# A new hand-written opening of six units, and a background planner with new costs, in a spectral filter plus gated MLP kernel

## The chip, the cores and the metric

The kernel runs on one core of a Trainium2 chip. The metric is the device time of one execution in microseconds (us); less is better. Engines are named as in the profile: PE is the matmul engine (TensorE), PEld its weight loads, DVE the vector engine, ACT the scalar engine, POOL the GpSimd engine, SP the engine whose queue issues the DMA transfers here.

## The reference

The input `x` has 2048 rows of 448. It is normalised along its rows, and three things are added: `x`, a filter in the frequency domain, and a gated MLP without bias.

```
xn = layernorm(x)                       # 2048 x 448
X  = rfft2(xn) * (w_r + 1j*w_i)         # 2048 x 225 complex
A  = irfft2(X, s=(2048, 448))
gate, up = xn @ W_gate, xn @ W_up       # 448 -> 1792
B  = (relu(gate) * up) @ W_down         # 1792 -> 448
out = x + A + B
```

## The kernel before

**Number format.** Every matrix product is made of fp16 products: an operand is split into a high part (its fp16 rounding) and a low part (the rest), and three products are summed: high by high, high by low, low by high. The low parts are made on DVE, most of the high parts on ACT. Weights are scaled by powers of two that come from their sums of squares: squares on ACT (`w_sq`, L661), the sum over partitions on POOL (`w_sum`, L666, a `partition_all_reduce`), the scale on DVE (`w_scale`, L671), then the high part on ACT (`w_hi`, L679) and the low part on DVE (`w_lo`, L683).

**Rows and chunks.** The 2048 rows are 16 blocks of 128, numbered n2. Four blocks form a chunk q (n2 = q, q+4, q+8, q+12); chunks are taken in the order 0, 2, 1, 3. A block is loaded (`load_xr`), its statistics taken on DVE (`ln_stats`), normalised, split into the tile `tt`, and transposed into `T{q}`, which holds the chunk with features on the partitions. For chunk 0 the transposes are matmuls with an identity (`ln_tp`, L328) into a PSUM tile `fx` and evictions (`ln_ev`, L334); for the others they are DMA transposes on the SP queue (`ln_dma`, L323).

**Units.** The hidden size 1792 is 14 slabs f of 128, in groups of 5, 5 and 4. A `gu` unit is one slab and one chunk: gate and up, 20 matmuls of 512 columns (`gu_full`, L728) and a pass of half-height matmuls that is shared by two units that stand next to each other, "mates" (`gu_halves`, L756). The unit's two PSUM tiles come from a ring of two (`gu`), so unit k+2 waits until unit k has been read. After it come relu on ACT (`gu_relu`), gate times up on DVE (`gu_times`), the high part of h on ACT (`gu_hi`) and the low part on DVE (`gu_lo`). When a group's slabs are done for a chunk, four `dn` units follow, one for each block: the down projection, 15 or 12 matmuls of 448 columns (`dn_mm`, L791), and an accumulation on DVE (`dn_post`, L803).

**The opening.** The first stretch is an order written by hand: the text `OPENING` (L30) is a list of pieces, and each piece's instructions go to their engines in that order, without any rescheduling. The names carry the work:

- `lx`, `ly`, `lw`, `lwd`, `lid`, `lfd`: transfers on SP of a block of x (for the norm, for the result), of the next weight slab, of a down slab, the identity, the DFT matrix
- `st`, `sq`/`rs`, `xn`, `hi`, `cp`, `lo`, `dm`: statistics; reciprocal root (A for blocks 0 and 4, B for 8 and 12, C for the second chunk); normalise; high part; a small copy on POOL; low part; DMA transpose
- `tpA`/`tpB`, `vev`/`aev`: three and five PE transposes of a block, and their eviction on DVE (v) or ACT (a)
- `wsq`, `par`, `wsc`, `whi`, `wlo`: the five weight steps, of slab `W0` to `W4`, gate `g0` and up `g1`
- `hh`, `lh`, `hl` with two digits: for slab 0, the products high by high, low by high and high by low, for gate or up (first digit) and one half of the chunk's columns (second digit, 256 columns)
- `gu1g0` and the like: a whole half unit, ten matmuls of 512 columns; `hp0`: the half-height pass of slab 0 and its mate
- `re`, `tm`, `gh`, `gl`: the four steps after a unit
- `wdq`, `wdp`, `wdsc`, `wdh`, `wdl`: the same steps for the down slabs
- `warm`, `kw1`, `kw3`, `kw6`: matmuls of 512 columns on a zeroed tile (`keep_warm`, L1052; `NWARM` = 19 for `warm`), whose result is not used

**After the opening** a loop goes over the unit list `units` (L989 to L998, L1147). A scheduler that simulates the engines sets the order in which the instructions stand in each engine's queue; units and their order in the list are priorities for it, not an order. Each unit is given weight steps and transfers at fixed distances before they are needed (`sched`, L1008 to L1046), and a share of the *background*: the list `bg` of all DFT steps, in order, each with a cost in us of DVE time and some with PE time (`PE_US`, L837). A unit may take background worth `room(i, share)`: its own length (`took`, L1121) times a share, less DVE work that it has anyway (`fixed`, L1124). The share is the smallest with which all the background fits (L1132 to L1138).

Of the kernel before, what the change touches and what calls it, by code (L numbers as in the profile page):

```python
# [30 lines left out]
lx0 lx4 lw lid lw lx8 lx12 lw lw lw lw lx2 lx10 lx6 lx14 lwd0 lwd1 lwd2 lwd3 lwd4 warm st0 st4 sqA rsA hi4  # L31
xn4 xn0 wsqW0g0 cp4 st8 hi0 parW0g0 st12 wsqW0g1 cp0 tpA0 lo0 tpA4 kw1 wscW0g0 sqB tpB0 kw6 parW0g1 wsqW1g0
rsB whiW0g0 vevB0 lo4 wsqW1g1 xn12 tpB4 kw3 hi8 parW1 wscW0g1 xn8 whiW0g1 cp8 vevA0 vevA4 hi12 tpA8 vevB4
hh10 hh00 lo8 wsqW2g1 cp12 tpA12 hl00 lo12 aevA12 tpB8 aevA8 hl10 wloW0g0 lw aevB8 tpB12 wscW1 lh00 aevB12
wloW0g1 lw lfd hh01 hh11 whiW1g0 st2 lh01 lh10 whiW1g1 hl01 wloW1g0 lw hl11 wsqW2g0 wloW1g1 lw ly0 ly4 ly8
ly12 lh11 wsqW3g0 st10 parW2 hp0 st14 wsqW3g1 gu1g0 st6 wdq0 parW3 wscW2 sqC wscW3 whiW2g0 rsC gu1g1 re0
wloW2g0 whiW3g1 tm0 whiW2g1 xn6 wsqW4g0 xn2 gu2g0 wloW2g1 hi2 re1 xn10 gh0 wloW3g1 whiW3g0 tm1 gu2g1 wdq1
wloW3g0 hi10 xn14 lo2 hi14 hi6 cp14 hp2 wsqW4g1 cp2 lo6 gu3g0 cp10 dm2 lo14 re2 parW4 wdq2 cp6 wscW4 tm2
whiW4g0 dm14 lo10 wdq4 gu3g1 wloW4g0 gh1 dm10 gl0 whiW4g1 gl1 dm6 gu4g0 re3 wloW4g1 wdq3 tm3 wdp gh3
wdsc gh2 gu4g1 gl2 wdh1 wdh2 wdl1 wdh0 wdl2 hp4 gl3 re4 wdh3 tm4 wdl0 gh4 wdh4 gl4 wdl3 wdl4  # L40
"""
# [41 lines left out]
def _constants():  # L83
# [49 lines left out]
    for r in (0, 2, 1, 3):  # L133
# [4 lines left out]
    c_fm = c_fm.reshape(4, 4, 128, 2, 128).transpose(1, 2, 0, 3, 4)  # L138
    ident = np.eye(128, dtype=np.float16)
    return dict(ident=ident, c_fd=c_fd, c_fm=np.ascontiguousarray(c_fm), c_im=c_im, c_row=c_row,  # L140
                c_id=np.ascontiguousarray(c_id))


@with_exitstack
def tile_gfnet_reglu(ctx: ExitStack, tc: tile.TileContext, x, xr, wgu, wd, wf, ident, c_fd, c_fm, c_im, c_row, c_id,
                     out):
# [181 lines left out]
    def ln_tp(n2, tiles):  # L328
        if n2 not in tp:
            tp[n2] = fx().bitcast(F16).rearrange("p (a b) -> p a b", b=128)  # L330
        for a in tiles:
            P.transpose(tp[n2][:, a, :], tt[n2][:, a, :], id_t)
# [394 lines left out]

    def gu_full(f, q, gs, cs, start, stop, seq=SEQ):  # L728
        for g in gs:
            for i, (a, b) in enumerate(seq):  # L730
                last["P"] = P.matmul(hps[f, q][:, g, cs], wt[f, g][:, a, :], Tq[q][:, b, cs],  # L731
                                     start=(start and i == 0), stop=(stop and i == len(seq) - 1)).ins

    def gu_half(f, q, g, start, prev):


        rows, b = TOP[g]
        m = P.matmul(hps[f, q][:, g, 0:512], wt[f, g][rows, 7, :], Tq[q][rows, b, :], start=start, stop=not start).ins  # L738
# [103 lines left out]
    def ln_chunk(q):  # L842
        for j in range(4):
            add(0.79, ln_stats, q, j)
        add(0.0, ln_sd, q)
        add(0.75, ln_rstd, q, (0, 1, 2, 3), True)
        n = [q + 4 * j for j in (0, 2, 1, 3)]
        for t in range(4 + 2):
            for st, (c, fn) in reversed(list(enumerate(((0.0, ln_norm), (0.78, ln_lo), (0.0, ln_dma))))):
# [5 lines left out]
    fl = ((0.0, f_dft), (0.77, f_eo), (1.08, f_x), (0.63, f_lo), (0.0, f_sdft), (None, f_y1))  # L855
    bf = (1.26, 2.04, 2.04, 2.04, 1.56, 2.04, 2.04, 2.04)

    def fft_chunk(q):
        n = [q + 4 * j for j in (0, 2, 1, 3)]
        for t in range(4 + len(fl) - 1):  # L860
            for st in reversed(range(len(fl))):
                i = t - st
                if 0 <= i < 4:
                    add(fl[st][0] if st < 5 else 1.25 * (n[i] >= 8), fl[st][1], n[i])

# [57 lines left out]
    for i0 in range(10):  # L923
# [15 lines left out]
        for k in pair_k:  # L939
            add(2.04, wmul, k)  # L940
# [76 lines left out]

    for f in groups[1] + groups[2]:
        s = first[f]
        for g in range(2):  # L1020
            sched(gslot(s, 7), w_sq, f, g)
        sched(gslot(s, 7), w_sum, f)
        sched(gslot(s, 5), w_scale, f)
        for g in range(2):
            sched(gslot(s, 4), w_hi, f, g)
            sched(gslot(s, 4), w_lo, f, g)
            sched(gslot(s, 4), load_wn)
    for i in range(8):
# [23 lines left out]
    def keep_warm(n):  # L1052
        for _ in range(n):
            P.matmul(wps, warm[:, 0:128], warm, start=True, stop=True)

    pieces = {"lid": lambda: nc.sync.dma_start(id_t, ident), "lfd": lambda: nc.sync.dma_start(fd_t, c_fd),
              "lw": load_wn, "warm": lambda: keep_warm(NWARM),
              **{f"kw{n}": (lambda n=n: keep_warm(n)) for n in (1, 3, 6)},
              "wdp": lambda: wd_sum(len(groups[0])),
# [24 lines left out]

    for f in groups[0]:
        piece(f"lwd{f}", load_wd, f)
        piece(f"wdq{f}", wd_sq, f, f)
        piece(f"wdh{f}", wd_hi, f, f)
        piece(f"wdl{f}", wd_lo, f, f)
        piece(f"parW{f}", w_sum, f)  # L1090
# [5 lines left out]
        for g in range(2):  # L1096
# [4 lines left out]
            if f == 0:  # L1101
                piece(f"parW{f}g{g}", w_sum, f, (g,))
                piece(f"wscW{f}g{g}", w_scale, f, (g,))
                for h in range(2):
                    for tag, sq in (("hh", seq1[0:3]), ("lh", seq1[3:6]), ("hl", seq2)):
                        piece(f"{tag}{g}{h}", gu_full, f, q, (g,), half[h], tag == "hh" and h == 0, False, sq)

    with tc.manual_schedule(engines={mybir.EngineType.PE, mybir.EngineType.DVE, mybir.EngineType.Activation,
                                     mybir.EngineType.SP, mybir.EngineType.Pool}):
        A.activation(mt([128, 1], F32, "root"), eps, AF.Sqrt)  # L1110
        G.memset(warm, 0.0)
        wps = psum.tile([128, 512], F32, name="dn", bufs=2)
# [33 lines left out]

    for i, u in list(enumerate(units))[len(groups[0]):-4]:  # L1147
        is_gu = u[0] == "gu"
# [7 lines left out]
        with after(LAG):  # L1156
# [6 lines left out]
            run_bg(amount=room(i, load[0]) if i >= RAMP else 0.0)  # L1163
        if is_gu:
# [57 lines left out]
```

## Time and profile before

| | |
|---|---|
| three timed runs | 446.81, 447.11, 447.32 us (median 447.11) |
| the profiled execution | 447.5 us, span 445.7 us |
| instructions | 7367 |
| busy, share of the span | PE 98%, DVE 87%, ACT 42%, POOL 6% |
| granted PE clock | full in all 40 slices |
| DMA | 39.54 MB, mean 89 GB/s |

The profile is of one execution. Its span runs from the first to the last instruction; the device time has some 2 us more around it. Lines such as L731 are lines of the kernel; a row of the timeline has the start in us from the span's start, the duration in us, the engine, the line, the operation, what it writes and reads, the count of instructions that were merged into the row, and in brackets the idle time of the engine before it and what ended it. A matmul's end is modelled and overlaps the next one's start, so the distance between starts says what a matmul costs.

### The profile page before, as it was taken

The numbers are of one execution on the slowest core, as the hardware profiler recorded it, in microseconds if no ns is written. First come the engines' busy times: TensorE is split into PE (matmuls) and PEld (weight loads), VectorE is DVE, ScalarE is ACT, GpSimd is POOL, SyncE is SP. The second block draws the span as 40 slices with busy tenths as digits, with TensorE's granted clock in tenths as the row PEclk, the third lists the DMA queues.
The fourth block names the chain that finished last, engine by engine and source line by source line (L and its number), as shares of the span: only waits on it lengthen the run. The fifth ranks groups of instructions, "written<-read, shape, count | busy, mean of one in ns | idle before, by whom it ended". The sixth has DMA issues, their size and how long they took to land.

```text
span 445.7 us, 7367 instructions
## 1 busy us (share of the span) xinstructions
PE 438.1 (98%) x2625; PEld 219.4 (49%) x2625; DVE 386.9 (87%) x958; ACT 187.0 (42%) x398; POOL 27.7 (6%) x77
## 2 busy tenths in 40 slices
PE   6999999999999999999999999999999999999997
PEld 2644645455445444444444444444454555555654
DVE  5999779786969999899999999999979799699753
ACT  4897263642552975133114354253323134144230
POOL 4220011200100040000000010000000000000000
PEclk9999999999999999999999999999999999999999
DMA  7919995400001272422220210002011211201212
GB/s 249 338 50 252 304 355 106 96 0 17 8 1 48 96 226 80 128 61 83 85 84 2 83 42 1 1 1 73 12 48 47 70 34 56 89 28 53 96 63 82
DMA packets 37756, 39.54 MB, mean 89 GB/s; under 512 B 16550, under 2 KB 33624, under 8 KB 37720
## 3 DMA queue, kind: packets, MB, share of 16 engines
q1 hardware_dynamic: 37720, 39.09, 28.3%
q8 instruction: 20, 0.33, 0.3%
q14 instruction: 16, 0.13, 0.1%
HBM read 24.38 MB, written 3.67 MB: 63 GB/s over the span
## 4 chain that ended last, share of the span: by engine, by line
PE 79%; DVE 9%; DMA 5%; ACT 3%; issue 1%; SPq 1%; DVEq 0%; ACTq 0%
PE gu L731 44%; PE dn L799 22%; PE gu L738 3%; PE fx L630 2%; PE fx L649 2%; PE fx L361 2%; PE fx L398 2%; DMA wf<-in_wf 1%; DMA sw<-y 1%; DMA y<-in_xr 1%; ACT junk L186 1%; PE dn L819 1%; ACT wt L681 1%; PE gu L819 1%; DVE wt L685 1%
## 5 line engine op out<-in xcount | busy, mean ns | idle before, releaser
L731 PE MATMUL gu<-T,wt 128*128 128x512 f16 (+1 forms) x1140 | 255.0, 375 | 0.0
L731 PEld LDWEIGHTS <-wt 128*128 128x128 f16 x1140 | 108.7, 98 | 128.7 <-issue 8.9
L799 PE MATMUL dn<-wdt,h 128*128 128x448 f16 x624 | 127.6, 353 | 0.1
L799 PEld LDWEIGHTS <-h 128*128 128x128 f16 x624 | 60.2, 98 | 57.7 <-issue 0.8
L768 ACT ACTIVATE g<-gu 128x512 f32<-128x512 f32 x56 | 33.0, 590 | 82.4 <-PE gu L738 55.6
L776 ACT ACTIVATE h<-g 128x512 f16<-128x512 f32 x56 | 35.1, 628 | 76.8 <-DVE g L772 73.8
L772 DVE SCALAR_TENSOR_TENSOR g<-gu,g 128x512 f32<-128x512 f32 x56 | 38.3, 684 | 4.2 <-ACT g L768 4.1
L780 DVE TENSOR_TENSOR h<-g,h 128x512 f16<-128x512 f32 x56 | 38.3, 685 | 3.7 <-ACT h L776 3.4
L805 DVE SCALAR_TENSOR_TENSOR xy<-dn,dsc,xy 128x448 f32<-128x448 f32 x44 | 29.9, 679 | 6.3 <-PE dn L799 6.2
L614 ACT ACTIVATE vt<-y,fsc 128x456 f16<-128x456 f32 x16 | 10.8, 673 | 26.1 <-PE fx L630 13.3
L654 DVE SCALAR_TENSOR_TENSOR xy<-fx,fsc,xy 128x448 f32<-128x448 f32 x16 | 10.8, 680 | 11.8 <-PE fx L649 11.7
L681 ACT ACTIVATE wt<-wst,wsc 128x512 f16<-128x512 f32 x28 | 19.2, 715 | 3.8 <-DVE wsc L196 3.8
L685 DVE SCALAR_TENSOR_TENSOR wt<-wst,wsc,wt 128x512 f16<-128x512 f32 x28 | 20.5, 747 | 0.1
L189 POOL PARTITION_ALL_REDUCE wm<-wm x15 | 7.8, 518 | 179.6 <-ACT junk L186 175.5
L186 ACT ACTIVATE junk<-wst 128x512 bf16<-128x512 f32 x28 | 17.5, 624 | 1.0 <-DMA wst<-in_wgu 0.7
L738 PE MATMUL gu<-T,wt 64*128 64x512 f16 x112 | 17.0, 381 | 0.2 <-DVE wt L685 0.2
L535 DVE TENSOR_TENSOR y<-y,sw 128x228 f32<-128x228 f32 x32 | 12.5, 390 | 5.0 <-DMA sw<-y 4.9
L405 DVE TENSOR_TENSOR y<-y,y 128x456 f32<-128x456 f32 x22 | 13.8, 629 | 1.7 <-DMA row<-y 1.4
L392 DVE TENSOR_TENSOR Xh<-X,Xh 128x456 f16<-128x456 f32 x16 | 10.0, 628 | 5.6 <-ACT Xh L389 5.5
L404 DVE TENSOR_TENSOR y<-y,y 128x456 f32<-128x456 f32 x22 | 13.9, 630 | 0.3
L389 ACT ACTIVATE Xh<-X 128x456 f16<-128x456 f32 x16 | 9.3, 578 | 10.1 <-DVE X L387 8.9
L630 PE MATMUL fx<-im,vt 128*128 128x128 f16 x192 | 13.4, 219 | 0.0
(130 smaller groups left out, 479.0 us busy)
## 6 DMA issues: line engine op xcount, KB each, us to landing
sw<-y SPq DMA_DIRECT2D x64, 112.2 KB
wst<-in_wgu SPq DMA_DIRECT2D x28, 256.0 KB
wf<-in_wf SPq DMA_DIRECT2D x16, 228.0 KB
y<-in_xr SPq DMA_DIRECT2D x16, 224.0 KB
xy<-in_x SPq DMA_DIRECT2D x16, 224.0 KB
out<-xy SPq DMA_DIRECT2D x15, 224.0 KB
wdst<-in_wd SPq DMA_DIRECT2D x14, 224.0 KB
fm<-in_c_fm SPq DMA_DIRECT2D x4, 256.0 KB
```

The source lines that it names most:

```text
L186: A.activation(mt([128, 512], BF16, "junk")[:, 0:src.shape[-1]], src, AF.Square, scale=SQ, accum_out=acc)
L630: P.matmul(o, v[:, h, w], m[:, c, :], start=(i == 0), stop=(i == 2), skip_group_check=True)
L681: A.activation(w[:, 0:4, :], wst[f, g], AF.Copy, scale=wsc[f, g])
L685: V.scalar_tensor_tensor(w[:, 4:8, :], st, sc, w[:, 0:4, :], op0=OP.mult, op1=OP.subtract)
L731: last["P"] = P.matmul(hps[f, q][:, g, cs], wt[f, g][:, a, :], Tq[q][:, b, cs], start=(start and i == 0), stop=(stop and i == len(seq) - 1 ...
L738: m = P.matmul(hps[f, q][:, g, 0:512], wt[f, g][rows, 7, :], Tq[q][rows, b, :], start=start, stop=not start).ins
L768: last["A"] = A.activation(g1s[f, q], hps[f, q][:, 0, :], AF.Relu, scale=2.0 ** -22).ins
L772: last["V"] = V.scalar_tensor_tensor(g1, hps[f, q][:, 1, :], 2.0 ** -22, g1, op0=OP.mult, op1=OP.mult).ins
L776: A.activation(ht[f, q][:, 0, :], g1s[f, q], AF.Copy)
L780: V.tensor_tensor(h[:, 1, :], g1s.pop((f, q)), h[:, 0, :], op=OP.subtract)
L799: last["P"] = P.matmul(ps[:, 0:D], ht[f, q][:, a, js], wdt[f][:, b, :], start=(i == 0), stop=(i == n - 1)).ins
L805: last["V"] = V.scalar_tensor_tensor(xy[:, n2, :], dps[n2][:, 0:D], dsc[:, g:g + 1], xy[:, n2, :], op0=OP.mult, op1=OP.add).ins
```

## The change

The opening is written in another order and holds more, and the planner gets other costs.

- The opening ends after six units instead of five: slab 5, the first of the second group, is done on chunk 0 in the opening (`ahead`). Its weights are loaded and split there (twelve `lw` instead of ten), and its h has a buffer of its own.
- Slab 1 is done as slab 0 is, in quarters of 256 columns: `ah`, `bh`, `ch` are for slab 1 what `hh`, `lh`, `hl` are for slab 0. The half pass `hp0` may now stand before the last quarters.
- The identity is no longer loaded: POOL makes it with a memset and an `affine_select`. The zeroed tile of the warm-up matmuls is set by DVE instead of POOL. There are 12 matmuls in `warm` instead of 19, and `kw1` and `kw9` instead of `kw1`, `kw6` and `kw3`.
- The transposes of block 8 use a PSUM buffer of the name `dn` instead of `fx`.
- Five of the pieces that evict transposes change their engine.
- The planner's DVE costs are lower (for instance 1.71 instead of 2.04 for a `wmul`), a `gu` unit counts as 4.62 us instead of 4.55, and `f_sdft` has 0.58 us of PE time instead of 1.14. Where a unit's own DVE work exceeds its share, the excess is now taken from the units before it (`rooms`); before, it was dropped.

```diff
-NWARM = 19
+NWARM = 12
 OPENING = """
...
+lx0 st0 lx4 st4 sqA lw wsqW0g0 lx12 rsA lx8 hi4 hi0 warm tpA4 kw1 tpA0 aevA4 lw lw parW0g0 st12 wscW0g0 st8 sqB
+xn0 xn4 wsqW0g1 whiW0g0 lw parW0g1 rsB aevA0 kw9 hh00 lo4 lw hi8 tpA8 cp0 wscW0g1 lo0 cp4 wloW0g0 hi12 lw tpB4
+vevB4 tpB0 tpA12 lh00 whiW0g1 hh10 vevB0 hl10 lw vevA12 lw wsqW1g0 wsqW1g1 wloW0g1 cp8 hl00 cp12 xn8 lh10 aevA8
+hh11 lw lh11 parW1 wscW1 hh01 lwd4 lh01 xn12 lo8 wsqW2g0 whiW1g1 whiW1g0 ah10 tpB8 ah00 lo12 tpB12 ch10 wsqW2g1
+lwd0 ah01 wdq0 wloW1g1 bh10 vevB8 vevB12 hl11 wsqW3g0 parW2 wscW2 hl01 ah11 wloW1g0 hp0 lx2 lx6 ly0 wsqW3g1 st2
+whiW2g1 bh01 bh11 parW3 wscW3 whiW2g0 re0 wloW2g1 lw bh00 wloW2g0 wsqW4g1 wsqW4g0 parW4 whiW3g0 tm0 ch11 lx10
+st6 st10 wloW3g0 whiW3g1 gh0 wscW4 lw lx14 lwd1 wloW3g1 ch00 lw st14 gu2g0 wsqW5g1 wdq4 ch01 gu2g1 re1 tm1 lwd2
+sqC whiW4g0 hp2 gu3g0 gh1 re2 rsC wsqW5g0 parW5 wloW4g0 xn6 xn2 hi2 xn10 hi10 hi6 tm2 wscW5 whiW5g1 cp10 gl1
+xn14 hi14 gl0 lo6 lo14 lwd3 ly8 wdq3 ly12 lo10 lfd whiW4g1 wloW4g1 cp2 gu4g0 whiW5g0 gu3g1 wloW5g0 lo2 ly4 wdq2
+re3 gu4g1 wdq1 cp6 dm6 tm3 wloW5g1 hp4 gu5g0 gh3 wdp gh2 wdsc wdh1 gl3 cp14 dm14 re4 gl2 gu5g1 wdl1 tm4 wdh4
+wdh3 wdl4 gh4 wdl3 dm10 wdh2 re5 dm2 gl4 wdl2 wdh0 tm5 wdl0 gh5 gl5
 """
...
     def ln_tp(n2, tiles):
         if n2 not in tp:
-            tp[n2] = fx().bitcast(F16).rearrange("p (a b) -> p a b", b=128)
+            t = fx() if n2 != 8 else psum.tile([128, 512], F32, name="dn", bufs=2)
+            tp[n2] = t.bitcast(F16).rearrange("p (a b) -> p a b", b=128)
...
-    PE_US = {"f_dft": 0.6, "f_sdft": 1.14, "i_sdft": 0.65, "i_ddft": 0.6, "row_dft": 0.2}
+    PE_US = {"f_dft": 0.58, "f_sdft": 0.58, "i_sdft": 0.7, "i_ddft": 0.57, "row_dft": 0.1}
...
-    bf = (1.26, 2.04, 2.04, 2.04, 1.56, 2.04, 2.04, 2.04)
+    bf = (1.09, 1.71, 1.71, 1.71, 1.23, 1.71, 1.71, 1.71)
...
     gseq = [("gu", g, f, q) for g, fs in enumerate(groups) for q in CHUNKS for f in fs]
+    ahead = ("gu", 1, groups[1][0], CHUNKS[0])
+    gseq.remove(ahead)
+    gseq.insert(len(groups[0]), ahead)
...
-        G.memset(warm, 0.0)
+        V.memset(warm, 0.0)
+        G.memset(id_t, 1.0)
+        G.affine_select(id_t, id_t, [[-1, 128]], OP.is_equal, 0.0, 0, 1)
...
-    took = lambda u: 4.55 if u[0] == "gu" else 0.56 * len(groups[u[1]])
-    V_US = {"w_scale": 0.33, "w_lo": 0.75, "wd_scale": 1.5, "wd_lo": 0.68}
+    took = lambda u: 4.62 if u[0] == "gu" else 0.56 * len(groups[u[1]])
+    V_US = {"w_scale": 0.3, "w_lo": 0.67, "wd_scale": 1.4, "wd_lo": 0.59}
 
     def fixed(i):
-        c = 1.37 if units[i][0] == "gu" else 0.68
+        c = 1.21 if units[i][0] == "gu" else 0.6
         return c + sum(V_US.get(fn.__name__, 0.0) for fn, a in at.get(i, []))
 
-    def room(i, share):
-        return max(0.0, share * took(units[i]) - fixed(i))
+    def rooms(share):
+        r, short = [0.0] * len(units), 0.0
+        for i in reversed(range(len(units))):
+            v = share * took(units[i]) - fixed(i) + short
+            r[i], short = max(0.0, v), min(0.0, v)
+        return r
...
-    for i, u in list(enumerate(units))[len(groups[0]):-4]:
+    for i, u in list(enumerate(units))[len(groups[0]) + 1:-4]:
```

More of the change, by code (lines that the diff above doesn't have):

```diff
@@ L30 @@
 OPENING = """
[L31 to L40, printed above, removed]
+lx0 st0 lx4 st4 sqA lw wsqW0g0 lx12 rsA lx8 hi4 hi0 warm tpA4 kw1 tpA0 aevA4 lw lw parW0g0 st12 wscW0g0 st8 sqB
[9 more added lines that the diff above has]
+wdh3 wdl4 gh4 wdl3 dm10 wdh2 re5 dm2 gl4 wdl2 wdh0 tm5 wdl0 gh5 gl5
 """
@@ L728, in gu_full @@
     def gu_full(f, q, gs, cs, start, stop, seq=SEQ):
+        if (f, q) not in hps:
+            gu_open(f, q)
         for g in gs:
@@ L732, in gu_full, with gu_half @@
                                      start=(start and i == 0), stop=(stop and i == len(seq) - 1)).ins
-    def gu_half(f, q, g, start, prev):
+    def gu_half(f, q, g, start, prev, stop):
         rows, b = TOP[g]
-        m = P.matmul(hps[f, q][:, g, 0:512], wt[f, g][rows, 7, :], Tq[q][rows, b, :], start=start, stop=not start).ins
+        m = P.matmul(hps[f, q][:, g, 0:512], wt[f, g][rows, 7, :], Tq[q][rows, b, :], start=start, stop=stop).ins
         if "opened" in state:
@@ L756, in gu_halves @@
     def gu_halves(f, q, mate):
-        gu_open(*mate)
+        fresh = mate not in hps
+        if fresh:
+            gu_open(*mate)
         m = last["P"]
@@ L848, in ln_chunk @@
         for t in range(4 + 2):
-            for st, (c, fn) in reversed(list(enumerate(((0.0, ln_norm), (0.78, ln_lo), (0.0, ln_dma))))):
+            for st, (c, fn) in reversed(list(enumerate(((0.0, ln_norm), (0.61, ln_lo), (0.0, ln_dma))))):
                 i = t - st
@@ L930, in tile_gfnet_reglu @@
         for k in pair_k:
-            add(0.78, pair, ("X", k), 1)
+            add(0.62, pair, ("X", k), 1)
         if i0 < 8:
@@ L1054, in keep_warm @@
             P.matmul(wps, warm[:, 0:128], warm, start=True, stop=True)
-    pieces = {"lid": lambda: nc.sync.dma_start(id_t, ident), "lfd": lambda: nc.sync.dma_start(fd_t, c_fd),
+    pieces = {"lfd": lambda: nc.sync.dma_start(fd_t, c_fd),
               "lw": load_wn, "warm": lambda: keep_warm(NWARM),
-              **{f"kw{n}": (lambda n=n: keep_warm(n)) for n in (1, 3, 6)},
+              **{f"kw{n}": (lambda n=n: keep_warm(n)) for n in (1, 9)},
               "wdp": lambda: wd_sum(len(groups[0])),
@@ L1083, in gu_slab @@
         gu_full(f, q, (g,), slice(0, 512), f % 2 == 0, f % 2 == 1)
[L1085 to L1089, printed above, removed]
+    for f in groups[0] + [ahead[2]]:
+        if f in groups[0]:
+            piece(f"lwd{f}", load_wd, f)
+            piece(f"wdq{f}", wd_sq, f, f)
+            piece(f"wdh{f}", wd_hi, f, f)
+            piece(f"wdl{f}", wd_lo, f, f)
         piece(f"parW{f}", w_sum, f)
@@ L1136, in tile_gfnet_reglu @@
         need = sum(c - m * p for c, p, _, _ in bg)
-        lo, hi = (m, hi) if sum(room(i, m) for i in range(RAMP, last_gu)) < need else (lo, m)
+        lo, hi = (m, hi) if sum(rooms(m)[RAMP:last_gu]) < need else (lo, m)
     load[0] = hi
+    room = rooms(hi)
     anchors, act_anchors = [last["V"]], [last["A"]]
```

33 lines of the change are left out of this document (17 added, 16 removed).

## The prediction

> **What bounds the kernel now.** I read the page first, then TensorE's waits, the sums by stretch, and the opening on each engine in order of time.
>
> ```profile
> PE 438.1 (98%) x2625; PEld 219.4 (49%) x2625; DVE 386.9 (87%) x958; ACT 187.0 (42%) x398; POOL 27.7 (6%) x77
> PE 79%; DVE 9%; DMA 5%; ACT 3%; issue 1%; SPq 1%; DVEq 0%; ACTq 0%
> ```
> ```profile
> PE dn L1054 <- POOL warm L1111: 3.6, 1, 3.6
> PE fx L332 <- ACT wt L681: 0.5, 1, 0.5
> PE gu L738 <- DVE wt L685: 0.2, 1, 0.2
> ```
> ```profile
> 10.00:20.00 10.00, 9.30 (x87) 6.65 (x86) 9.64 (x32) 9.17 (x20) 1.91 (x6) 1.00 0.96 357
> 20.00:30.00 10.00, 10.00 (x50) 4.14 (x47) 9.19 (x26) 9.32 (x23) 0.93 (x5) 1.00 0.29 94
> ...
> 250.00:300.00 50.00, 50.00 (x251) 22.96 (x250) 49.13 (x116) 21.41 (x49) 4.17 (x6) 1.00 0.08 23
> ```
>
> TensorE (first number after the length of the stretch) is the bound: its three listed waits all lie before 20 us, and it is full in both later stretches. DVE (third) is close behind: 9.64 of 10 in the opening, 49.13 of 50 later. So nothing that comes after the opening can be made shorter; a later stretch can only be made worse. What can be won is the time before TensorE becomes dense:
>
> ```profile
> 3.58 6.86 PE L1054 MATMUL dn<-warm 128*128 128x512 f16 x19 [3.58 <-POOL warm L1111]
> 10.27 0.50 PE L332 MATMUL fx<-id_t,tt 128*128 128x128 f16 x6
> ...
> 14.36 0.81 PE L731 MATMUL gu<-T,wt 128*128 128x256 f16 x6
> ...
> 15.18 0.60 PE L731 MATMUL gu<-T,wt 128*128 128x256 f16 x4
> 15.61 0.44 PE L332 MATMUL fx<-id_t,tt 128*128 128x128 f16 x5
> ...
> 19.88 0.60 PE L738 MATMUL gu<-T,wt 64*128 64x512 f16 x4 [0.18 <-DVE wt L685]
> ```
> ```profile
> 38.44 0.60 PE L738 MATMUL gu<-T,wt 64*128 64x512 f16 x4
> 38.97 4.49 PE L731 MATMUL gu<-T,wt 128*128 128x512 f16 x20
> 43.30 0.54 PE L799 MATMUL dn<-wdt,h 128*128 128x448 f16 x2
> 43.68 2.32 PE L731 MATMUL gu<-T,wt 128*128 128x512 f16 x10
> ```
>
> The first useful matmul starts at 14.36. At 43.30 TensorE has done six units: the five of the opening and the next (20 matmuls from 38.97, so 4.33 a unit, 0.216 a matmul). The pass of four half matmuls costs 38.97 - 38.44 = 0.53. The changed kernel's opening also ends after six units, so 43.30 is the mark to compare with.
>
> **The change part by part.**
>
> *Warm-up.* Nineteen matmuls took 10.27 - 3.58 = 6.69, against 4.1 at 0.216; if some ran at double, 0.43, it was twelve of them, about 5.2 us. Now twelve run, 5.2 us, and start when DVE has zeroed the tile instead of GpSimd:
>
> ```profile
> 3.00 0.53 POOL L1111 MEMSET warm<- 128x512 f16 x1
> ...
> 3.27 0.63 DVE L250 BATCH_NORM_STATS2 bst<-y 128x6 f32<-128x448 f32 x1 [2.40 <-DMA y<-in_xr]
> ```
>
> DVE idles 2.40 there, so the memset (0.1 to 0.6 by the GpSimd row) hides, and the warm-up runs from about 1.4 to 6.5. The seven matmuls saved are worth nothing by themselves: before, TensorE waited for data right behind them. The identity's memset and select follow on GpSimd from 3.0; with 0.5 for the one and anything up to 3 us for the other they end before 6.9, the first transpose's time (below). If they took longer, each further us would be lost whole, and GpSimd's first weight sum, queued behind, would be late too.
>
> *The order on DVE.* This sets the opening's end. Costs are distances between starts, since instructions overlap a little:
>
> ```profile
> 8.42 0.63 DVE L250 BATCH_NORM_STATS2 bst<-y 128x6 f32<-128x448 f32 x1 [1.42 <-DMA y<-in_xr]
> ...
> 9.18 0.59 DVE L250 BATCH_NORM_STATS2 bst<-y 128x6 f32<-128x448 f32 x1
> ...
> 10.48 0.15 DVE L192 TENSOR_SCALAR eg<-wm 128x1 uint32<-128x1 uint32 x1
> ...
> 10.74 0.15 DVE L266 RECIPROCAL rs<-rs 128x2 f32<-128x2 f32 x1
> ...
> 11.59 0.48 DVE L340 COPY T<-fx 128x640 f16<-128x640 f16 x1
> 11.99 0.55 DVE L317 TENSOR_TENSOR tt<-y,tt 128x384 f16<-128x384 f32 x1
> ...
> 12.59 0.51 DVE L293 TENSOR_SCALAR y<-y,mv,rs 128x448 f32<-128x448 f32 x1
> 13.02 0.15 DVE L192 TENSOR_SCALAR eg<-wm 128x1 uint32<-128x1 uint32 x1
> ...
> 15.90 0.74 DVE L685 SCALAR_TENSOR_TENSOR wt<-wst,wsc,wt 128x512 f16<-128x512 f32 x1
> 16.56 0.15 DVE L192 TENSOR_SCALAR eg<-wm 128x2 uint32<-128x2 uint32 x1
> ```
> ```profile
> 23.83 0.69 DVE L772 SCALAR_TENSOR_TENSOR g<-gu,g 128x512 f32<-128x512 f32 x1
> 24.43 0.51 DVE L293 TENSOR_SCALAR y<-y,mv,rs 128x448 f32<-128x448 f32 x1
> ```
>
> So: statistics (st) 0.75, weight scale (wsc) 0.26, reciprocal root (rs) 0.85, eviction of five tiles (vevB) 0.40, low part of the input (lo) 0.60, normalise (xn) 0.43, low part of a weight (wlo) 0.66, gate times up (tm) 0.60; the low part of h (gl), of the same shape, is taken as 0.60, the eviction of three tiles (vevA) as 0.3.
>
> Everything hangs on chunk row 8, which st8 waited for at 8.42.
>
> ```profile
> 2.13 0.43 SPq L1056 DMA_DIRECT2D id_t<-in_ident  x1
> ...
> 3.08 0.91 SPq L220 DMA_DIRECT2D y<-in_xr  x2
> ```
>
> It was the sixth transfer, issued at 3.08; without the identity, and with row 12 in place of the second weight slab ahead of it, it is the fifth, one step of 0.47 earlier: st8 starts at 8.0 (bounds 7.3, if the queue ahead drains faster, and 8.42, if nothing is gained).
>
> From there DVE is packed. Up to wloW0g0: st8 0.75, xn0 and xn4 0.86, rsB 0.85, lo4 and lo0 1.20, wscW0g1 0.26, wloW0g0 0.66: 4.6, to 12.6. Then to wloW5g1: three vevB 1.2 and one more 0.4 (vevB4, B0, B8, B12), vevA12 0.3, eleven wlo 7.3, six xn 2.6, five wsc 1.3, six lo 3.6, four st 3.0, rsC 0.8, four tm 2.4, two gl 1.2: 24.1, to 36.7, and about 0.4 where a tm waits for its relu. So the weights of unit 5 are whole at 37.1. Behind them TensorE has only the half pass hp4 (0.53) and unit 5 (4.33): it ends the opening at **42.0**.
>
> *TensorE's own order.* ACT waits for st8, then does a root (0.3), the squares of W0g1 (0.6), the high part of W0g0 (0.7) and the eviction of row 0 (about 0.5, as DVE's 0.48 for more tiles), so the first useful matmul goes at 10.9 instead of 14.36:
>
> ```profile
> 4.88 0.29 ACT L261 ACTIVATE rs<-mv,eps 128x2 f32<-128x2 f32 x1 [2.64 <-DVE mv L253]
> ...
> 6.19 0.76 ACT L300 ACTIVATE tt<-y,rs 128x448 f16<-128x448 f32 x1 [1.01 <-DVE rs L271]
> 6.85 0.62 ACT L186 ACTIVATE junk<-wst 128x512 bf16<-128x512 f32 x1
> ...
> 10.85 0.72 ACT L681 ACTIVATE wt<-wst,wsc 128x512 f16<-128x512 f32 x1
> ```
>
> The squares of W0g0 move into the gap ahead of 6.19; tpA4 comes at about 6.9. Dense work starts at 13.2, once vevB4 (12.6 + 0.48) frees a PSUM buffer for tpA12: 28 us remain then (six units 26.0, three half passes 1.6, two tpB 0.6, less 0.3 done), which would end at 41.1. The DVE chain's 42.0 is later and counts. Of the 3.5 us won on the first matmul 1.3 remain at the mark. Quartering the second pair: four matmuls of 256 columns took 15.61 - 15.18 = 0.43, as two of 512 do; nothing.
>
> *The second chunk's transposes.* They now come last:
>
> ```profile
> 30.71 5.43 SPq L326 DMA_TRANSPOSE T<-tt  x4
> ```
>
> Each holds SP 1.36. GpSimd copies row 14 only after the down weights' sum, which waits for wdq1 behind re3 on ACT (unit 3 ends at 34.5, one slab of 2.17 and a short wait before hp4): re3 0.5, wdq1 0.7, sum 0.45, copy 0.4 give 36.6; dm14, dm10, dm2 follow and the last is issued at 39.3. Before, the last was issued at 34.8 and its data was in use at 38.44, at most 3.65 later; at least the 1.36 of its own issue passes. So unit (0, chunk 2) can start between 40.7 and 43.0, against a free TensorE at 42.0: a cost of 0 to 1.0. I take 0.3, as the true landing must lie inside the 3.65.
>
> *Background.* The planner's sum, done with the new costs, lowers the share from 1.05 to 0.89 of a unit's time and spreads short units backwards; weighed with the distances above, the largest DVE backlog over the units falls from 1.9 to 0.8 us. As TensorE did not wait after 20 us, this is worth 0; if it went wrong it costs (below).
>
> Sum: 43.3 - 42.0 - 0.3 = 1.0 less. The profiled execution took 447.5 (span 445.7), so 446.5 on its scale; the three timed runs have a median of 447.11, and there it is **446.1**.
>
> **The rivals.** A measurement tells about 0.2% here, 0.9 us.
>
> *The gain slips away on DVE.* Before, DVE once stood for GpSimd, and a cover of TensorE work hid it:
>
> ```profile
> 31.77 0.17 DVE L192 TENSOR_SCALAR eg<-wm 128x2 uint32<-128x2 uint32 x1 [0.33 <-POOL wm L189]
> ```
>
> Now TensorE waits for DVE at hp4 without cover, so a slip of that kind, with st8 at 8.4 or transposes at 43.0, takes 0.4 to 1.0: 446.2 to 447.1, centre 446.7.
>
> *The clock stays low.* Twelve warm-up matmuls are just what ran at double time before. If the low rate lasts, kw9 ends at 11.6, hh00 and the transposes double, vevB4 comes 0.9 late and later pieces lose 0.5 more: 447.5. For it: idle gaps from 6.5 on, and an exact fit. [...]
>
> *Slower: down projection first.* If TensorE's queue has the down matmuls of row 0 ahead of unit (0, chunk 2), they wait for wdl0. DVE from 37.1: scaling 1.7 (ten small instructions at 0.17, as the five of rsB took), gl3, gl2, gl4 1.8, tm4, tm5 1.2, five wdl 2.9: 44.7. TensorE stands 2.7 us: 447.1 - 1.3 + 2.7 = 448.5. It decides from the place in the queue alone. For it: the unit list now has the down rows straight behind six units. Against: the rows at 43.30 and 43.68 show that the queue leaves the list (two down matmuls, ten of a later unit, then down again).
>
> *Slower: a DVE pile-up later.* 49.13 of 50 leaves little; a few instructions of 0.65 placed too early in front of a gate would stop TensorE by 1 to 2.5: 447.1 to 448.6.
>
> **How the numbers follow.** The forecast with its own range 445.3 to 446.2: 0.42. Slip: 0.28. Clock: 0.08. Down first: 0.12. Pile-up: 0.10, of which 0.08 slower. So faster 0.42, same 0.38 (slip, clock and the rest), slower 0.20. The range 445.2 to 448.4 leaves out the two slower cases' ends.
>
> **What would show it.** Right: warm-up from 1.4; st8 at 8.0; first gu at 10.9; hp4 at 37.1 behind a wait for DVE wt; TensorE past six units at 42.0 to 42.3; no wait afterwards. Wrong: a wait of dn for wdt near 42, warm pace of 0.43 past 10, or waits of gu or dn after 50 us.

## The result, and the profile after

The changed kernel takes **461.88 us** (median of 6 runs, 458.40 to 462.22) against 447.06 for the kernel before, measured beside it (6 runs, 446.61 to 447.32): a ratio of 1.032, 95% interval 1.029 to 1.035. The forecast was 446.1, with a range to 448.4. The profiled execution took 462.04 us, its span 460.3.

The page of the kernel after, its engines and its chain of waits:

```profile
PE 441.7 (96%) x2638; PEld 222.6 (48%) x2638; DVE 390.0 (85%) x960; ACT 186.3 (40%) x397; POOL 27.2 (6%) x78
PE 90%; issue 4%; DVE 4%; ACT 1%; POOL 1%; POOLq 0%; ACTq 0%
```

TensorE's share fell from 98% to 96%, and in the chain "issue", time in which an engine waited for nothing that the profile shows, rose from 1% to 4% of 460 us, some 18 us. TensorE's waits (total, times, longest):

```profile
PE fx L333 <- POOL id_t L1124: 8.7, 1, 8.7
PE gu L734 <- ACT T L339: 4.5, 1, 4.5
PE dn L1062 <- DVE warm L1122: 1.3, 1, 1.3
PE gu L741 <- DVE wt L686: 0.5, 1, 0.5
```

The first is new: the first transposes wait 8.7 us for the identity. GpSimd in order of time (start, duration, idle before and what ended it in brackets):

```profile
3.06 0.21 POOL L1123 MEMSET id_t<- 128x128 f16 x1
15.01 0.28 POOL L1124 TENSOR_SCALAR_AFFINE_SELECT id_t<-id_t 128x128 f16<-128x128 f16 x1 [11.73 <-issue]
21.40 0.40 POOL L189 PARTITION_ALL_REDUCE wm<-wm  x1 [6.11 <-issue]
```

In the kernel before, the first weight sum came at 7.65, right behind its input:

```profile
7.65 0.40 POOL L189 PARTITION_ALL_REDUCE wm<-wm  x1 [0.25 <-ACT junk L186]
```

The select itself takes 0.28 us, but GpSimd stands still for 11.73 us ahead of it and for another 6.11 ahead of the first weight sum, both "issue": 17.8 us together, and most of what the chain lists. What hangs on the sum, on DVE:

```profile
7.59 0.63 DVE L250 BATCH_NORM_STATS2 bst<-y 128x6 f32<-128x448 f32 x1 [1.19 <-DMA y<-in_xr]
...
21.84 0.15 DVE L192 TENSOR_SCALAR eg<-wm 128x1 uint32<-128x1 uint32 x1 [13.40 <-POOL wm L189]
...
22.10 0.62 DVE L250 BATCH_NORM_STATS2 bst<-y 128x6 f32<-128x448 f32 x1
```

DVE has row 12's statistics done by 8.3 and then stands for 13.40 us at the weight scale; row 8's statistics (st8), which need nothing from it, are queued behind and start at 22.10. And TensorE:

```profile
1.30 5.30 PE L1062 MATMUL dn<-warm 128*128 128x512 f16 x12 [1.30 <-DVE warm L1122]
15.35 0.48 PE L333 MATMUL fx<-id_t,tt 128*128 128x128 f16 x3 [8.75 <-POOL id_t L1124]
...
24.91 0.80 PE L734 MATMUL gu<-T,wt 128*128 128x256 f16 x3 [4.50 <-ACT T L339]
...
53.22 0.60 PE L741 MATMUL gu<-T,wt 64*128 64x512 f16 x4 [0.49 <-DVE wt L686]
53.76 8.46 PE L734 MATMUL gu<-T,wt 128*128 128x512 f16 x38
```

The sixth unit begins at 53.76; with 4.33 us a unit, six units are done at 58.1 instead of 43.30, 14.8 later. What remains behind that mark is 460.3 - 58.1 = 402.2 us, against 445.7 - 43.3 = 402.4 before. The whole loss lies in the opening.

### The profile page after: what moved, and what is told of

It reads as the page before. It is cut to its first block, busy times and chain, and to the rows that moved or that the text cites. A ratio compares the mean times of both kernels' runs of the same rounds, so it can differ in the third digit from the quotient of the medians.

```text
span 460.3 us, 7398 instructions
## 1 busy us (share of the span) xinstructions
PE 441.7 (96%) x2638; PEld 222.6 (48%) x2638; DVE 390.0 (85%) x960; ACT 186.3 (40%) x397; POOL 27.2 (6%) x78
## 4 chain that ended last, share of the span: by engine, by line
PE 90%; issue 4%; DVE 4%; ACT 1%; POOL 1%; POOLq 0%; ACTq 0%
PE gu L734 50%; PE dn L804 26%; PE gu L741 3%; PE fx L631 2%; PE fx L362 2%; PE fx L650 2%; PE fx L399 2%; PE dn L824 1%; DVE wt L686 1%; PE gu L824 1%; DVE tt L317 1%; ACT junk L186 1%; DVE y L293 1%; POOL Tl L280 0%; DVE g L777 0%
## 5 line engine op out<-in xcount | busy, mean ns | idle before, releaser
L734 PE MATMUL gu<-T,wt 128*128 128x512 f16 (+1 forms) x1160 | 257.6, 374 | 4.5 <-ACT T L339 4.5
L734 PEld LDWEIGHTS <-wt 128*128 128x128 f16 x1160 | 111.7, 98 | 133.6 <-issue 10.7
L189 POOL PARTITION_ALL_REDUCE wm<-wm x15 | 6.6, 442 | 159.7 <-ACT junk L186 147.0
L192 DVE TENSOR_SCALAR eg<-wm 128x2 uint32<-128x2 uint32 (+1 forms) x15 | 2.4, 157 | 13.4 <-POOL wm L189 13.4
```

## The experiments

Theory S: the select brings both idles on GpSimd, 11.73 us before itself and 6.11 before the first weight sum, and all later work waits. Rival O: the opening's order is too tight in itself. Rival P: the new pacing harms. Each ratio below is to the kernel before, run in the same session, with its 95% interval in brackets.

### The identity by transfer again: e1_lid4 and e2_lid6

```diff
-lx0 st0 lx4 st4 sqA lw wsqW0g0 lx12 rsA lx8 hi4 hi0 warm ...
+lx0 st0 lx4 st4 sqA lw lid wsqW0g0 lx12 rsA lx8 hi4 hi0 warm ...   # e1
+lx0 st0 lx4 st4 sqA lw wsqW0g0 lx12 rsA lx8 lid hi4 hi0 warm ...   # e2
-        G.memset(id_t, 1.0)
-        G.affine_select(id_t, id_t, [[-1, 128]], OP.is_equal, 0.0, 0, 1)
```

> The changed kernel with one part undone: the identity is loaded by a transfer again, fourth in SP's queue as before, and GpSimd makes none. [...] Rival O (the new order is too tight, whatever makes the identity): waits of TensorE for DVE and ACT of 3 us or more stay, time 449 to 455. Rival P (the new pacing costs): six units done by 43 but waits of gu or dn after 60 us, time 448 to 452.

> As e1_lid4, but the identity's transfer stands sixth, behind block 8's, so it delays neither block 12 nor block 8. Theory S: st8 at 7.6 as in the changed kernel (8.0 in the forecast), six units done at 41.7 to 42.6, time 445.6 to 446.6, 0.2 to 0.6 less than e1_lid4, unless the first transposes, which need the identity at about 6.9 to 8.3, come late. Rival O: 449 to 455. Rival P: 448 to 452, with waits after 60 us.

e1_lid4: 447.93 us (446.38 to 450.05), ratio 1.0021 [1.0007, 1.0035]. e2_lid6: 447.60 (446.41 to 448.73), 1.0014 [1.0000, 1.0027]. Without the select nearly all of the loss is gone, though both medians lie above what S had forecast (446.0 to 447.0 and 445.6 to 446.6). TensorE in e1_lid4, whose profiled execution took 446.38 (span 444.6):

```profile
7.02 0.34 PE L334 MATMUL fx<-id_t,tt 128*128 128x128 f16 x3 [0.49 <-ACT tt L301]
...
10.41 0.49 PE L735 MATMUL gu<-T,wt 128*128 128x256 f16 x3 [0.46 <-ACT T L340]
...
13.17 3.65 PE L735 MATMUL gu<-T,wt 128*128 128x256 f16 x32
...
37.22 0.60 PE L742 MATMUL gu<-T,wt 64*128 64x512 f16 x4 [0.48 <-DVE wt L687]
37.76 9.08 PE L735 MATMUL gu<-T,wt 128*128 128x512 f16 x40
```

This is the forecast's opening: first gate/up matmul at 10.4, dense from 13.2, the half pass at 37.2 behind a wait for DVE, six units done at 37.76 + 4.33 = 42.1. Rival O in its strong form falls. But this execution is the fastest of twelve, and their median is 1.6 us above it: the new opening's executions have a standard deviation of 1.0 us, those of the kernel before 0.5.

### The select alone in the kernel before: e3_before_select

```diff
         G.memset(warm, 0.0)
+        G.memset(id_t, 1.0)
+        G.affine_select(id_t, id_t, [[-1, 128]], OP.is_equal, 0.0, 0, 1)
```

The transfer `lid` is taken out; all else is the kernel before.

> The kernel before with this one part of the change: no identity transfer, GpSimd makes the identity by memset and affine_select behind its other memsets. Theory S: GpSimd idle about 11.7 us before the select and about 6 us before the first partition sum; the first copies and sums come at about 15 and 21 us instead of 7.0 and 7.7; the first gu matmul at 25 to 28 instead of 14.4, time 457 to 461. Rivals O and P: the select is cheap here, time 446.5 to 448.

460.25 us, ratio 1.030 [1.028, 1.032].

```profile
14.93 0.28 POOL L1112 TENSOR_SCALAR_AFFINE_SELECT id_t<-id_t 128x128 f16<-128x128 f16 x1 [11.19 <-issue]
...
21.59 0.40 POOL L188 PARTITION_ALL_REDUCE wm<-wm  x1 [6.01 <-issue]
```

The same two idles, 11.19 and 6.01, in the old order: this one edit costs 13.2 us, of 14.8 for the whole change.

### Who waits for it: e5_lid4_sel

e1_lid4 with the memset and the select left in their place, on a tile that nobody reads.

> The kernel after with the identity again by transfer, fourth in SP's queue, but the memset and the select left in their place on GpSimd, on a tile that nobody reads. PE no longer waits for the select; GpSimd still passes through it before the first weight sum. [...] If PE's wait for the identity were the loss: 447 to 449 us.

462.38 us, in one execution, where S had 459 to 462. The first transposes come at 7.1, yet

```profile
13.75 0.28 POOL L1126 TENSOR_SCALAR_AFFINE_SELECT sel_t<-sel_t 128x128 f16<-128x128 f16 x1 [10.47 <-issue]
19.93 0.40 POOL L190 PARTITION_ALL_REDUCE wm<-wm  x1 [5.91 <-issue]
```
```profile
PE gu L736 <- ACT T L341: 13.4, 1, 13.4
```

TensorE's wait moved from the identity to the next thing, 13.4 us in one piece. The largest line in the list of waits (8.7 us for `id_t`) was thus not what set the time: GpSimd's queue was, through the weight sum.

### Only the order of two GpSimd instructions: e6_sum_first

One more all-reduce, of a scratch column, is put ahead of the select. S, made sharper, says that the order of the two costs: no idle of 11.7 and none of 6 here, and 446.4 to 448.0 us, against 458 to 462 if the select brings the idles in any order.

```diff
         G.memset(id_t, 1.0)
+        G.memset(one, 0.0)
+        G.partition_all_reduce(one, one, 128, bass_isa.ReduceOp.add)
         G.affine_select(id_t, id_t, [[-1, 128]], OP.is_equal, 0.0, 0, 1)
```

> The kernel after with one more instruction: an all-reduce over partitions of a scratch column of zeros (128 x 1) on GpSimd right before the select. [...] If the order of the opening were too tight by itself (rival O): above 449 us even with the identity in time.

448.96 us, ratio 1.0043 [1.0026, 1.0060]: 12.9 us less than the kernel after, for one added all-reduce and the memset of its column. That is 1 us above the range that S gave and just under the 449 of rival O; the later runs ask what is left over.

```profile
3.44 0.40 POOL L1126 PARTITION_ALL_REDUCE one<-one  x1
3.72 0.36 POOL L1127 TENSOR_SCALAR_AFFINE_SELECT id_t<-id_t 128x128 f16<-128x128 f16 x1
7.44 0.39 POOL L189 PARTITION_ALL_REDUCE wm<-wm  x1 [3.36 <-ACT junk L186]
```

No idle before the select, and none on "issue" before the weight sum. S holds in the sharper form as far as the order goes: behind an all-reduce the select is there at once; ahead of the first one it costs both waits. The second waits, 6.11, 6.01 and 5.91, agree with each other; the first ones, 11.73, 11.19 and 10.47, are nearly twice that, and no run here shows why. Nor does a trace show what GpSimd does in them: from 15.4 to 21.3 us, in the second idle of the kernel after, the DMA engines were busy for 0.00 of the time, and the pages of the kernel before, the kernel after and e6_sum_first list the same transfers of instructions (20 and 16 packets).

### How much was the clock: e7_keepwarm

52 warm-up matmuls instead of 12 and 38 instead of the later 9.

> The kernel after with 52 warm-up matmuls instead of 12 and 38 in place of the later 9, so that PE does not idle while it waits for the select. [...] S: the first weight sum still at about 21.4, and only what the low clock cost is won back: in the kernel after, the 27 transposes and first matmuls between 15 and 28 us ran at 0.5 to 0.7 of the clock, so 1 to 2.5 us less, 459.4 to 460.9 us. If the loss were mostly the clock: 450 to 455 us.

461.38 us, with a granted clock of 0.999 or 1.000 in each execution. The median is 0.5 below that of the kernel after, under the 1 to 2.5 that I had expected, and against the runs beside it the ratio is the same 1.032 [1.030, 1.033]. The two profiled executions differ by more: the sixth unit starts at 52.58 here and at 53.76 in the kernel after, 1.2 later. The executions of the kernel after spread over 3.8 us, so the size stays rough, but by either figure it is small beside 14.8. The waits decide.

### The pacing: e8_before_newplan and e4_lid6_oldplan

The planner's constants and `rooms` put into the kernel before, and the old ones into e2_lid6.

> The kernel before, its opening and its transfer of the identity untouched, with the planner's new costs, its new duration of a unit and its new rooms (background paced by occupied time). My prediction put the pacing at nothing: 446.8 to 447.3 us. Rival P1 (the new pacing is worth time in itself, as the 4.7 us between the two kernels with the new opening suggest): 443 to 446 us. Rival P2 (it is the cause of the spread from 446.4 to 450 us seen with the new opening): the same median, and executions spread over 2 us or more.

> e2_lid6 with the planner's costs, the unit length and the room rule of before: the opening is the same, only the background is paced as before. Theory S with the forecast's reading (pacing is worth 0, TensorE waits for nothing after 60 us in either): within 0.4 us of e2_lid6. Rival P: 1.5 to 5 us faster than e2_lid6. If pacing helps after all: 0.5 to 3 us slower than e2_lid6, with waits of gu or dn between 60 and 430 us.

e8_before_newplan: 446.75 us (446.46 to 447.21), ratio 0.9991 [0.9982, 0.9999]. e4_lid6_oldplan: 452.27 (450.89 to 454.89), 1.0126 [1.0102, 1.0150], 4.7 above e2_lid6, more than any of its three cases allowed. The waits of TensorE that it has from 150 to 300 us and e2_lid6 has not:

```profile
PE gu L735 <- DVE g L778: 2.7, 2, 1.6
PE dn L805 <- ACT h L782: 0.6, 1, 0.6
PE dn L805 <- DVE xy L811: 0.4, 1, 0.4
```

They make 3.7 of the 4.1 us by which its span is longer (449.1 against 445.0).

Rival P falls: the pacing is worth 0.3 us with the old opening, barely clear of noise, and it is what keeps the new opening from waiting, mostly for DVE. e8_before_newplan is the only version here whose interval lies below 1.

### The spread of the new opening: e9, e10, e11

ScalarE's first weight square, `wsqW0g0`, now stands ahead of the norms and waits for a transfer:

```profile
5.59 0.63 ACT L187 ACTIVATE junk<-wst 128x512 bf16<-128x512 f32 x1 [0.43 <-DMA wst<-in_wgu]
```
```profile
6.62 0.63 ACT L186 ACTIVATE junk<-wst 128x512 bf16<-128x512 f32 x1 [1.23 <-DMA wst<-in_wgu]
```

The first is e1_lid4's profiled execution (446.38 us), the second e6_sum_first's (447.94). Three kernels move that square behind `hi4 hi0`: e9_dma_move on e1_lid4, e10_gp_move on e6_sum_first, and e11_gp_move_warm with 15 warm-up matmuls.

```diff
-... sqA lw wsqW0g0 lx12 rsA lx8 hi4 hi0 warm ...
+... sqA lw lx12 rsA lx8 hi4 hi0 wsqW0g0 warm ...
```

> The kernel of e1_lid4 (identity by transfer) with one step moved in the order: ScalarE squares the first weight tile (wsqW0g0) after the two norms hi4 and hi0 instead of ahead of them, as the kernel before has it. Theory A (the spread of the new opening is the landing of the first weight tile: ScalarE waits for it with the norms, and so PE's first transposes, queued behind; the wait was 0.43 us in e1_lid4's trace, 0.95 in e2_lid6's, 1.23 in e6_sum_first's, 1.52 in the kernel after's, and past about 1 us of PE's idle the nine warm-up matmuls behind run at half clock, 3.6 to 3.8 us instead of 2.1): the wait is gone, transposes at 6.9 to 7.2, first gate/up matmul at 10.4 to 11.2, executions within 1 us of each other, median 446.2 to 446.8. Rival B (another transfer jitters, such as the x tiles of the second pair or the later slabs): the spread of 446.4 to 450 and the median of 447.9 stay.

> The kernel of e6_sum_first (identity on GpSimd, after an all-reduce of a scratch column) with the same move of wsqW0g0 behind hi4 and hi0. Theory A: as e9_dma_move or a little better, since one transfer less lies ahead of the x tiles: median 446.0 to 446.8, executions within 1 us. Rival B: 448 to 449.5 us with the spread of e6_sum_first (447.9 to 450.5).

> e10_gp_move with 15 warm-up matmuls instead of 12 (three more, 0.43 us each while the clock is low, 0.22 after), so that PE idles less ahead of the first transposes. Theory A and e10: if the norms come at 7 us, the three end at 6.8 to 7.4 and cost 0 to 0.3 us; if they come later, they keep the nine behind at full clock. 446.0 to 447.0 us, within 0.3 of e10_gp_move. Rival B: nothing gained over e10_gp_move.

The "about 1 us" in theory A is an estimate: TensorE idled 0.49 us ahead of its first transposes in e1_lid4, 1.93 in e2_lid6 and 1.94 in e6_sum_first, and the nine warm-up matmuls behind took 2.10, 3.55 and 3.79 us.

450.21, 450.52 and 450.03 us: 1.0063 [1.0047, 1.0079], 1.0076 [1.0063, 1.0089], 1.0064 [1.0052, 1.0076]. All are slower than theory A allowed. Rival B's ranges were missed too, but for its "nothing gained" on e11_gp_move_warm. DVE and TensorE of e9_dma_move:

```profile
8.87 0.15 DVE L193 TENSOR_SCALAR eg<-wm 128x1 uint32<-128x1 uint32 x1 [1.49 <-POOL wm L190]
...
9.13 0.62 DVE L251 BATCH_NORM_STATS2 bst<-y 128x6 f32<-128x448 f32 x1
```
```profile
11.94 0.49 PE L735 MATMUL gu<-T,wt 128*128 128x256 f16 x3 [1.96 <-ACT T L340]
```

The sum comes later, st8 waits behind the scale, and the first gate/up matmul slips from 10.41 to 11.94: in small, what the late sum did in the kernel after. The slip is not all. In these three traces the 32 matmuls that come next, 3.65 us in e1_lid4, took 4.44, 6.16 and 6.43 us, at a granted clock of 0.80, 0.51 and 0.50 from 14 to 20 us: up to 2.8 us more.

### Both orders undone: e12, e13, e14

```diff
-... parW0g0 st12 wscW0g0 st8 sqB
+... parW0g0 st12 st8 wscW0g0 sqB
```

e12_gp_move_st8 is e11 with this; e13_dma_move_st8 the same with the identity by transfer; e14_gp_st8 leaves the square ahead of the norms and has 18 warm-up matmuls.

> e11_gp_move_warm (identity on GpSimd after a scratch all-reduce, wsqW0g0 behind the norms, 15 warm-up matmuls) with one more step moved: on VectorE the statistics st8 stand ahead of the weight scale wscW0g0. Theory C (what the later weight sum cost in e9_dma_move, e10_gp_move and e11_gp_move_warm is that st8 stands behind the weight scale in VectorE's order: the sum came at 8.4 us instead of 6.5, st8 at 9.1 instead of 7.6, the square root behind it on ScalarE at 10.0 instead of 8.5, and the first gate/up matmul at 11.9 instead of 10.4): st8 at 7.2 to 7.7, no wait of 2 us, first gate/up matmul at 10.4 to 11.0, six units at 42.1 to 42.7, median 446.0 to 447.3 and executions within 1 us of each other. Rival D (the weight's own chain, sum, scale, high part, sets the first matmul): it stays at 11.5 to 12 and the time at 449 to 450.

> The same three edits with the identity by transfer, fourth in SP's queue, instead of on GpSimd. Theory C: within 0.5 us of e12_gp_move_st8, 446.0 to 447.5. If the identity's place (one transfer more ahead of the x tiles against a select on GpSimd) matters, a difference of 0.5 to 1 us between the two.

> e6_sum_first with st8 ahead of the weight scale and 18 warm-up matmuls instead of 12, the square of the first weight tile left ahead of the norms. Theory C and the landing of that tile: ScalarE still waits for it, 0.4 to 1.5 us from one execution to another, but the warm-ups keep the clock up and the weight scale no longer holds st8: the first gate/up matmul at 10.5 to 11.7, median 446.8 to 448.2, spread 1 to 2 us, 0.5 to 1.5 slower than e12_gp_move_st8. If the spread has nothing to do with that tile: both spread alike.

448.34 (1.0028 [1.0014, 1.0041]), 448.59 (1.0022 [1.0009, 1.0036]) and 447.38 us (1.0004 [0.9995, 1.0013]). Theory C holds for the step: the first gate/up matmul is back at 10.55 in e12. It fails for the total: e12 and e13 lie above their ranges. e14 lies inside its own, but it was to be slower than e12 and is faster. e12 and e13 have almost the same opening, but (start, duration):

```profile
13.73 3.65 PE L735 MATMUL gu<-T,wt 128*128 128x256 f16 x32
```
```profile
13.95 5.17 PE L735 MATMUL gu<-T,wt 128*128 128x256 f16 x32
```

and, in the sums by stretch (PE, PEld, DVE, ACT, POOL, then the granted clock, the DMA share and GB/s), e12 ahead of e13:

```profile
14.00:20.00 6.00, 6.00 (x63) 5.43 (x61) 5.86 (x17) 5.44 (x16) 1.41 (x2) 1.00 0.94 307
```
```profile
14.00:20.00 6.00, 6.00 (x49) 4.82 (x47) 4.57 (x13) 5.29 (x14) 1.56 (x2) 0.75 0.95 310
```

The same 32 matmuls take 1.5 us longer in e13, because the clock granted from 14 to 20 us was 0.75 instead of 1.00.

By the microsecond, e13's clock was 0.81 from 13 to 14 us, 0.50 from 14 to 17, 0.98 from 17 to 18 and 1.00 behind: 3.4 us at half rate. In slices of 0.2 us over the first 62 us, every low spell of the kept traces is that long or a multiple: 3.41 in e2_lid6, e4_lid6_oldplan, e6_sum_first, e9_dma_move and e13_dma_move_st8, 6.83 in e10_gp_move and e11_gp_move_warm, 10.24 and 6.83 in the kernel after, 13.65 in e3_before_select, 17.07 in e5_lid4_sel. What parted e12 from e13 no run here shows. The length of one idle did not: between its first matmul and its spell TensorE never idled longer than 0.80 us in e13, and in e12, without a spell, it idled 0.78.

### PE kept at work: e15, e16, e17

```diff
-... aevA0 kw9 hh00 lo4 ... vevB4 tpB0 tpA12 lh00 ...
+... aevA0 kw9 hh00 kw2 lo4 ... vevB4 tpB0 kw3 tpA12 lh00 ...
```

On e14 (e15_gp_fill), on e1_lid4 with 18 warm-up matmuls (e16_dma_fill), and on the latter with st8 ahead of the scale (e17_dma_st8_fill).

> e14_gp_st8 with five more warm-up matmuls: two behind the first gate/up triple and three ahead of the last transposes of the first chunk, where PE idles 0.4 to 0.8 us each. Theory E (the rest of the loss and the spread is TensorE's clock: after the idles between 7 and 14 us it falls in some executions, and the matmuls that come then run at half rate for 3 to 4 us: the 32 first dense ones took 5.17 us in e13_dma_move_st8's trace and 3.65 in e12_gp_move_st8's, the nine warm-ups 3.79 in e6_sum_first's and 2.10 in e1_lid4's, 1.5 to 1.7 us each time): with PE kept at work the clock stays, every execution is a good one, median 446.2 to 446.8 and the spread under 1 us. Rival F (transfers that land at other times): the median and spread of e14_gp_st8 stay (447.4, 446.5 to 448.1), or 0.1 to 0.3 more for the five matmuls.

> e1_lid4 (identity by transfer, order of the kernel after) with 18 warm-up matmuls instead of 12 and the same five. Theory E: the spread of 446.4 to 450.0 shrinks to about 1 us plus what the first weight tile's landing still moves (it stands ahead of st8 on VectorE and of the norms on ScalarE), median 446.5 to 447.2 instead of 447.9. Rival F: 447.5 to 448.3 as before.

> e15_gp_fill with the identity by transfer, fourth in SP's queue. Theory E: as e15_gp_fill within 0.3 us. If the transfer ahead of the x tiles costs: 0.3 to 0.8 us more.

447.62 (1.0015 [1.0004, 1.0025]), 447.51 (1.0005 [0.9995, 1.0015]) and 447.25 us (0.9999 [0.9989, 1.0010]). The clock was 1.00 in every stretch of the three traces, and 0.999 or 1.000 in each of the 34 executions. Theory E fails all the same: no median lies in its range (that of e17 misses by 0.07), and rival F's figures came for e15 and e16. The standard deviation is 0.7 us in each, with 0.4 for the kernel before, 1.0 for e1_lid4 and 0.5 for e14_gp_st8. Against e1_lid4 the fill and six more warm-up matmuls of e16_dma_fill may have won some 0.4 us in the median; the intervals overlap. On e14_gp_st8 the fill won nothing.

Nor is it the clock that spreads the executions of the earlier versions, for the mean granted clock of each is on record; one spell of 3.4 us brings it to about 0.996. In e1_lid4 three of twelve have that, 447.54 to 448.10 us, and the nine with 0.999 or 1.000 run from 446.38 to 450.05. In e2_lid6 the seven with a spell (446.41 to 447.80) are all faster than the five without (448.30 to 448.73). Of the twelve of e13_dma_move_st8 only the profiled one has it, and its 448.59 is the median. (The record leaves out the start: the first 12 matmuls of e1_lid4 took 5.30 us, 0.44 each, while it says 1.00.)

The traces of e1_lid4 and e16_dma_fill show a possible part, the second chunk's transposes on SP's queue:

```profile
33.25 7.33 SPq L327 DMA_TRANSPOSE T<-tt  x4
```
```profile
33.36 8.52 SPq L327 DMA_TRANSPOSE T<-tt  x4
```
```profile
43.75 4.48 PE L735 MATMUL gu<-T,wt 128*128 128x512 f16 x20 [1.38 <-DVE wdt L719]
```

Four transposes from nearly the same start are through 1.2 us later in e16_dma_fill: the third held SP for 2.41 us, the others for 1.24 to 1.36. The first unit of that chunk (last row) waits 1.38 us, where in e1_lid4 the starts leave 0.28 (46.68 - 37.76, less 40 matmuls at 0.216). The row names a DVE instruction that those matmuls don't read; they read the transposed tile. In e15_gp_fill the four took 7.83, in the other fourteen traces with this opening 7.33 to 7.41. What remains open is where the spread comes from: the transposes are seen late in two profiled executions, not counted over many.

## Why the prediction was wrong

**The step that failed** is the price of the identity on GpSimd: "with 0.5 for the one and anything up to 3 us for the other they end before 6.9". The select ended at 15.3. The 0.5 was the row of a memset; behind the 3 us stands no row, and no row of the trace before showed a select at all. The sentence behind it ("each further us would be lost whole, and GpSimd's first weight sum, queued behind, would be late too") named the path, and e5_lid4_sel showed the sum to be the part that counts: the identity alone came 8.4 us after 6.9, and 14.8 were lost. But it got no rival and no chance. Of the 15.8 us between forecast and result, 12.9 are these two waits (e6_sum_first); the other 2.9 are what e6_sum_first still lies above the forecast.

**The rest of the opening's sum** agrees with one execution with the identity in time, the fastest of e1_lid4:

| step | forecast | e1_lid4 |
|---|---|---|
| st8 on DVE | 8.0 (7.3 to 8.42) | 7.59 |
| first gate/up matmul | 10.9 | 10.41 |
| dense from | 13.2 | 13.17 |
| weights of unit 5 (half pass) | 37.1 | 37.22 |
| wait for chunk 2's transposes | 0.3 (0 to 1.0) | 0.28 |
| gain on the span | 1.0 | 445.7 - 444.6 = 1.1 |

Part of this is luck. By the medians e1_lid4 is 0.9 us slower than the kernel before, not 1.0 faster, and in the traces of e2_lid6 and e6_sum_first the first gate/up matmul came at 11.90 and 12.51, the half pass at 37.64 and 38.26. Nor did st8 come at 7.59 for the reason given, a transfer one step earlier: in e1_lid4 it starts without a wait, behind row 12's statistics and the weight scale.

**What the sum left out** is that these steps stand in a chain with little slack, so that a late input counts: a weight sum 2 us later moved the first gate/up matmul by 1.5 us and the half pass by 2.4, 0.8 of it at low clock (e9_dma_move), and the median of e1_lid4 is 1.6 above its profiled execution. The transposes reached 1.38, beyond my bound of 1.0. What spreads the executions stays open. Undoing one order and adding six warm-up matmuls (e6 to e14) took 448.96 to 447.38; their shares were not parted.

**"Background: worth 0"** was nearly right for the old opening (0.3) and wrong for the new one (4.7). The reason given, that TensorE did not wait after 20 us, was a fact of the old opening only: with the new one and the old costs it waited 3.7 us.

**The rivals.** None of the priced ones decided the time. "The clock stays low" was real in part: half rate cost 1.5 us in the trace of e13_dma_move_st8 and up to 2.8 in that of e11_gp_move_warm; in the kernel after it was worth 0.5 by the medians and 1.2 between two traces (e7_keepwarm). No run bears out a chance as low as the 0.08 given to it: the low rate held for most of kw9 in e2_lid6 and e6_sum_first, 3.55 and 3.79 us against 2.10 in e1_lid4. "Down projection first" and the later pile-up did not occur in the changed kernel; with the old costs (e4_lid6_oldplan) the pile-up did.

## What to carry to other kernels

An operation that the trace does not show has no upper bound from rows of other operations of that engine: give "it costs far more" a chance, above all if the engine's queue carries something that everyone waits for. When a big wait is named in the list, ask what stands behind it in the same queue before you remove it; here the wait for the identity could go altogether with no gain. Look for idle marked "issue", and try another order of the two instructions around it: here an all-reduce ahead of the select was worth 12.9 us. Whether other pairs on GpSimd behave so, no run here shows.

## What the runs showed of the hardware

- A select ahead of GpSimd's first all-reduce: 10.5 to 11.7 us of idle before it and 5.9 to 6.2 before the all-reduce, in four kernels. The same select behind an all-reduce: 0.36 us, no idle.
- TensorE's granted clock in a low spell: 0.50, for 3.41 us or a multiple of it up to 17.07, in ten traces. After nearly equal idles of at most 0.8 us behind the first matmul it was 1.00 in one trace and 0.75 in another from 14 to 20 us, 3.65 against 5.17 us for the same 32 matmuls.
- One DMA transpose held SP's queue for 1.23 to 1.36 us; in two traces one of four took 1.71 and 2.41.
